# One key tile of 128 rows with quadrant scores, four load buffers, and loads issued two steps further ahead, in an mLSTM and mixture-of-experts kernel

## The chip, the cores and the metric

The kernel runs on one core of one Trainium2 chip. A core has five engines that run their own instruction streams in order: TensorE (PE in the rows; PEld is its weight load), VectorE (DVE), ScalarE (ACT), GpSimd (POOL) and SyncE (SP), which here issues nearly all loads and stores. The metric is the device time of one execution in microseconds (us), lower is better. Times are medians of several runs; the rows come from one profiled execution.

## The reference, cut to what matters

For 4 batches, 8 heads, 768 tokens and a head dimension of 40, a matrix memory is carried from token to token, read with q, gated and normalised. The result, 3072 tokens of 320 features, goes to a mixture of 8 experts where each token takes the one with the largest cosine logit.

```python
for t in range(768):                       # per batch and head
    m_new = max(f[t] + m, i[t])
    C = exp(f[t]+m-m_new) * C + exp(i[t]-m_new) * outer(v[t], k[t])
    n = exp(f[t]+m-m_new) * n + exp(i[t]-m_new) * k[t]
    y[t] = sigmoid(o[t]) * (C @ q[t]) / max(abs(n @ q[t]), 1)
x = y.reshape(3072, 320)                   # heads side by side
logits = unit(x) @ unit(expert_emb).T / tau
e = argmax(logits);  gate = softmax(logits)[e]
out = gate * (relu(x @ w1[e]) @ w2[e])     # w1: 320x1024, w2: 1024x320
```

## The kernel before

The recurrence is computed by chunks of 64 tokens. The loop over n has 24 steps: 6 windows of 128 tokens, each for 4 batches, so one step is 128 tokens of one batch, that is two chunks c of 64 tokens, for 8 heads. Two steps are a pair q and share one load of keys (transposed, `k_e` and `k_o`), one of queries (`q_s`, transposed) and two of rows (`kv_s`, one per step, with keys and values token by token). Each of these has three buffers (NB).

The order of the work is the order of the code, engine by engine; a framework adds only the semaphores. On PE a step n does, in this order:
- stage_add for chunk 0 (L664 carries the state in, L674 adds keys times weighted values) into the PSUM tile `y`. ACT then copies the state between the chunks out of it (`c_mid`, L690, two copies).
- stage_scores of the next step (L637): for each chunk and head a product of 64 keys and 64 queries over 40 dimensions. Heads of even and of odd position sit in two tiles, `k_e` and `k_o`, each of 128 partitions of which 40 are loaded and the rest hold zeros, so that a product over all 128 partitions picks one head out of `q_s`, where two heads sit at partitions 0 to 39 and 64 to 103. The scores `s` of a step fill one PSUM bank; DVE multiplies them with the causal mask into `w_s` (L646).
- stage_y: scores times values (L712), which comes behind ACT's `c_mid` because both touch the bank of `y`; on odd steps five transposes (L792, `px` and `pj`) for the router; and queries times state (L725).
- stage_add for chunk 1 (L674), and on odd steps the logits of an earlier pair (L812, `pm`).

Beside it DVE computes denominators, outputs and the router's argmax in small pieces (L743 to L1009), POOL the weighted values `uv` (L622) and the output gate (L762), ACT copies and squares (L785, L771, L798), and from step 10 on ACT and DVE or POOL split the first expert's weights into two parts (`w1h`, L197, from the loaded tile `raw`). After the loop the mixture of experts (L390, L428) runs, PE-bound, to the end.

Loads are issued in step n by SP in this order: k of pair (n+4)/2 on even steps or q on odd steps, rows, the output gates `sig`, from step 10 on weights `raw` (W_AT), and late in the step the store of an output tile (`x_d`, L766), which waits for POOL's gate. The framework gives the transfers eight semaphores in turn (DMAHW0 to DMAHW7), so each waits until the one eight before it has landed.

Before the loop, the unloaded partitions of six key tiles are zeroed by DVE, POOL and ACT (L1087). PSUM is full: one bank each for `s` (pS), `pj` (pJ) and `px` (pX), two for the router's and the gates' small products (pM), three for `y` (pY).

Of the kernel before, what the change touches and what calls it, by code (L numbers as in the profile page):

```python
# [11 lines left out]
F32 = mybir.dt.float32  # L12
# [11 lines left out]
E, F = 8, 1024  # L24
# [26 lines left out]
W_AT = (10, 12, 13, 15, 16, 18, 19, 20, 22, 22, 22, 23, 23)  # L51
W2_AT = (4, 6, 8, 10, 11, 13, 14)
# [14 lines left out]
def tile_mlstm_moe(  # L67
# [149 lines left out]
    pM = mctx.enter_context(tc.tile_pool(name="pM", bufs=2, space=PSUM))  # L217
# [90 lines left out]
    turns = [(pM, "pm"), (pX, "px")]  # L308
# [229 lines left out]
    with ExitStack() as actx:  # L538
# [7 lines left out]
        pS = ictx.enter_context(tc.tile_pool(name="pS", bufs=1, space=PSUM, side="right"))  # L546
        pJ = ictx.enter_context(tc.tile_pool(name="pJ", bufs=1, space=PSUM, side="right"))

# [12 lines left out]
        NH, NG, NB = B * H, NJ * B * H, 3  # L561
# [11 lines left out]
        k_e, k_o, q_s, kv_s, kr_s, vr_s, uv, w_s = [], [], [], [], [], [], [], []  # L573
        for i in range(NB):
# [5 lines left out]
            vr_s.append(kv_s[i][:, :, :, :, D:])  # L580
            uv.append(ap1.tile([P, 2, NP, 2, D1], F32, name=f"uv{i}"))
            w_s.append(ap1.tile([P, 2, NP, L], F32, name=f"w_s{i}"))
# [11 lines left out]
        def stage_row(q, k, eng=SY):  # L594
            eng.dma_start(
                kv_s[q % NB][:, k].rearrange("p c a d -> p (c a d)"), rows_in[q][:, k].rearrange("p c a d -> p (c a d)")
            )

        def stage_k(q, ks=slice(0, 2)):
            for r, kk in ((0, k_e), (1, k_o)):  # L600
                SY.dma_start(
                    kk[q % NB][r * L : r * L + D, ks].rearrange("d n a t -> d (n a t)"),
                    kt[q, r][:, ks].rearrange("d n a t -> d (n a t)"),
                )

        def stage_q(q, ks=slice(0, 2)):
            SY.dma_start(
                q_s[q % NB][:, ks].rearrange("d n a t -> d (n a t)"), qt[q][:, ks].rearrange("d n a t -> d (n a t)")
# [8 lines left out]
        def stage_uv(n, eng=None):  # L617
            q, k = divmod(n, 2)
            j, b = divmod(n, B)
            for r in range(2):  # L620
# [3 lines left out]
                    vr_s[q % NB][rows, k],  # L624
# [4 lines left out]
        def stage_scores(n):  # L629
            q, k = divmod(n, 2)  # L630
            s = st.setdefault(n, {})["s"] = pS.tile([P, 2, NP, L], F32, name=f"s_{n}", tag="ps")
            for c in range(2):
                cs = slice(c * L, c * L + L)
                for a in range(NP):
                    for r in range(2):
                        m = a // 2 * 2 + r
                        T.matmul(  # L637
                            s[r * L : r * L + L, c, a],
                            (k_e, k_o)[a % 2][q % NB][:, k, m, cs],
                            q_s[q % NB][:, k, m, cs],  # L640
                            start=True,
                            stop=True,
                        )

        def stage_weigh(n):
            V.tensor_tensor(  # L646
                w_s[n % NB].rearrange("p c a t -> p (c a) t"),
                st[n]["s"].rearrange("p c a t -> p (c a) t"),
                late.unsqueeze(1).broadcast_to([P, 2 * NP, L]),
# [6 lines left out]
        def stage_add(n, c):  # L656
# [15 lines left out]
            for a in range(NP):  # L672
# [3 lines left out]
                    kr_s[q % NB][:, k, c, a],  # L676
# [28 lines left out]
        def stage_y(n, mid=None):  # L705
# [4 lines left out]
            for a in range(NP):  # L710
                for c in range(2):
                    T.matmul(  # L712
                        y[c * L : c * L + L, a * 2 * D1 : (a + 1) * 2 * D1],
                        w_s[n % NB][:, c, a],
# [7 lines left out]
            for m in range(NP):  # L722
                for c, state in ((0, c_st[n % B]), (1, c_mid[n % 2])):
                    if n >= B or c:
                        T.matmul(  # L725
                            yp[c * L : c * L + L, m // 2, :, m % 2],
                            q_s[q % NB][:, k, m, c * L : c * L + L],
# [73 lines left out]
        def stage_logits(q):  # L801
# [4 lines left out]
            if b == 0:  # L806
                grp[g] = dict(pm=pM.tile([P, 512], F32, name=f"pm_{g}", tag="pm"))
            xt = st.pop(n)["xt"]
            st.pop(n + 1)
            for c in range(NX):  # L810
                for r0 in (0, L):
                    T.matmul(  # L812
                        grp[g]["pm"][r0 : r0 + L, b * E : (b + 2) * E],
# [23 lines left out]
        def pmv(g, k):  # L837
# [1032 lines left out]
```

## Time and profile before

| what | value |
|---|---|
| device time, median of 3 runs | 327.11 us (326.43 to 327.32) |
| the profiled execution | 328.47 us |
| its span, first to last instruction | 326.7 us |
| PE busy | 307.4 us (94%) |
| DVE, ACT, POOL busy | 217.2, 164.1, 146.4 us |
| DMA: data, mean rate | 58.52 MB, 179 GB/s |

The span is what the page's shares refer to; 1.8 us of the profiled execution lie outside it. "Idle before" of an instruction is the time that its engine stood before it, with the engine or transfer that ended the wait. A group in a timeline (x16) has the time from its first start to its last end; in the chain of waits, pieces that follow each other don't overlap, so their lengths add up. Matmul records: an instruction in 32-bit floats leaves two records, so the 16 products of one step's scores are "x32".

### The profile page before, as it was taken

The numbers are of one execution on the slowest core, as the hardware profiler recorded it, in microseconds if no ns is written. First come the engines' busy times: TensorE is split into PE (matmuls) and PEld (weight loads), VectorE is DVE, ScalarE is ACT, GpSimd is POOL, SyncE is SP. The second block draws the span as 40 slices with busy tenths as digits, with TensorE's granted clock in tenths as the row PEclk, the third lists the DMA queues.
The fourth block names the chain that finished last, engine by engine and source line by source line (L and its number), as shares of the span: only waits on it lengthen the run. The fifth ranks groups of instructions, "written<-read, shape, count | busy, mean of one in ns | idle before, by whom it ended". The sixth has DMA issues, their size and how long they took to land.

```text
span 326.7 us, 9770 instructions
## 1 busy us (share of the span) xinstructions
PE 307.4 (94%) x3769; PEld 290.8 (89%) x3769; DVE 217.2 (66%) x631; ACT 164.1 (50%) x431; POOL 146.4 (45%) x182
## 2 busy tenths in 40 slices
PE   8998999989988879999999999999999999999991
PEld 3787999978876779999999999999999999999990
DVE  5776797897775549796567684574585584766520
ACT  4656556655663695344265463263373463555300
POOL 6659777688784297040635302321251321512121
PEclk9999999999999979999999999999999999999998
DMA  7998797998997523030594964446446465411001
GB/s 228 283 342 252 264 306 238 290 321 272 340 340 219 183 55 113 2 80 3 180 328 168 316 187 134 129 131 191 124 105 247 112 198 198 129 48 42 10 26 33
DMA packets 25101, 58.52 MB, mean 179 GB/s; under 512 B 3707, under 2 KB 10056, under 8 KB 25046
## 3 DMA queue, kind: packets, MB, share of 16 engines
q1 hardware_dynamic: 22166, 48.91, 47.0%
q0 software_dynamic: 2624, 8.48, 8.4%
q8 instruction: 31, 0.51, 0.7%
q10 hardware_dynamic: 256, 0.43, 0.4%
q14 instruction: 24, 0.20, 0.2%
HBM read 49.98 MB, written 8.19 MB: 178 GB/s over the span
## 4 chain that ended last, share of the span: by engine, by line
PE 84%; DVE 4%; DMA 4%; ACT 4%; issue 2%; POOL 1%; POOLq 0%; DVEq 0%; ACTq 0%
PE ph L390 29%; PE po L428 17%; PE s L637 4%; PE po_b L428 4%; PE po_a L428 4%; PE y L712 4%; PE y L674 3%; PE y L725 3%; PE po L415 3%; PE pt L351 2%; PE warm L1078 2%; DMA k_o<-in_kt 2%; PE pm L812 2%; PE px L792 2%; DMA raw<-in_w 2%
## 5 line engine op out<-in xcount | busy, mean ns | idle before, releaser
L447 POOL DMA_INDIRECT out<-ob,ids x20 | 20.3, 1015 | 99.2 <-DVE ob L444 73.7
L622 POOL TENSOR_TENSOR uv<-kv_s,u_t 64x328 f32<-64x328 f32 x47 | 35.3, 751 | 12.7 <-PE y L674 5.4
L428 PE MATMUL po<-w2h,hh 128*128 128x320 f32 x128 | 40.3, 315 | 0.0
L392 ACT ACTIVATE hh<-ph 128x448 fp32r<-128x448 f32 (+2 forms) x48 | 23.7, 493 | 32.7 <-PE ph L390 29.8
L428 PE MATMUL po<-w2h,hl 128*128 128x320 f32 x128 | 39.6, 309 | 0.0
L428 PE MATMUL po<-w2l,hh 128*128 128x320 f32 x128 | 39.5, 309 | 0.0
L394 DVE SCALAR_TENSOR_TENSOR hl<-ph,hh 128x384 fp32r<-128x384 f32 (+1 forms) x48 | 24.5, 511 | 14.6 <-ACT hh L392 12.3
L390 PE MATMUL ph<-xh,w1l 128*128 128x448 f32 (+2 forms) x96 | 32.0, 337 | 0.0
L390 PE MATMUL ph<-xh,w1h 128*128 128x448 f32 (+2 forms) x96 | 32.0, 336 | 0.0
L197 ACT CAST w1h<-raw 128x512 fp32r<-128x512 f32 x48 | 28.9, 616 | 5.4 <-DMA raw<-in_w 4.9
L444 DVE TENSOR_SCALAR ob<-po,gts 128x320 f32<-128x320 f32 x16 | 8.8, 551 | 27.8 <-PE po L428 27.8
L200 DVE TENSOR_TENSOR w2l<-raw,w2h 128x320 fp32r<-128x320 f32 x58 | 26.7, 497 | 0.2
L197 ACT CAST w2h<-raw 128x320 fp32r<-128x320 f32 x64 | 26.1, 461 | 0.0
L637 PE MATMUL s<-q_s,k_e 128*64 128x64 f32 x384 | 24.5, 223 | 1.2 <-DVE w_s L646 1.2
L690 ACT COPY c_mid<-y 40x164 f32<-40x164 f32 x48 | 14.0, 293 | 22.0 <-PE y L674 21.6
L637 PE MATMUL s<-q_s,k_o 128*64 128x64 f32 x384 | 24.5, 222 | 0.5 <-issue 0.5
L390 PE MATMUL ph<-xl,w1h 128*128 128x448 f32 (+2 forms) x96 | 24.6, 337 | 0.0
L312 POOL DMA_INDIRECT xs<-x_d,ids x20 | 21.4, 1070 | 6.9 <-issue 5.5
L200 DVE TENSOR_TENSOR w1l<-raw,w1h 128x512 fp32r<-128x512 f32 x36 | 24.4, 687 | 0.0
L428 PEld LDWEIGHTS po<-w2l,hh 128*128 128x128 f32 x128 | 24.1, 188 | 0.0
L428 PEld LDWEIGHTS po<-w2h,hh 128*128 128x128 f32 x128 | 24.1, 188 | 0.0
L428 PEld LDWEIGHTS po<-w2h,hl 128*128 128x128 f32 x128 | 24.0, 188 | 0.0
(327 smaller groups left out, 922.2 us busy)
## 6 DMA issues: line engine op xcount, KB each, us to landing
raw<-in_w SPq DMA_DIRECT2D x21, 512.0 KB
raw<-in_w SPq DMA_DIRECT2D x32, 320.0 KB
kv_s<-in_rows SPq DMA_DIRECT2D x23, 324.0 KB
q_s<-in_qt SPq DMA_DIRECT2D x11, 512.0 KB
sig<-in_og SPq DMA_DIRECT2D x24, 160.0 KB
x_d<-x SPq DMA_DIRECT2D x24, 160.0 KB
k_e<-in_kt SPq DMA_DIRECT2D x11, 160.0 KB
k_o<-in_kt SPq DMA_DIRECT2D x11, 160.0 KB
```

The costliest lines, as they stand in the source:

```text
L197: A.copy(h, src)
L200: (eng or V).tensor_tensor(lo, src, h.bitcast(F32), ALU.subtract)
L312: G.indirect_dma_start(out=xs[0 : c.shape[0], a, 0:DM], out_offset=None, in_=x_d[0:rows], in_offset=bass.IndirectOffsetOnAxis(ap=c, axis=0 ...
L390: T.matmul(ph, lt, rh, start=i == 0, stop=i == len(ops) - 1)
L392: A.activation(hh, ph, AF.Relu)
L394: V.scalar_tensor_tensor(hl[:, 0:full], ph[:, 0:full], 0.0, hh[:, 0:full].bitcast(F32), ALU.max, ALU.subtract)
L428: T.matmul(po[0 : ts_.stop - ts_.start, 0:DM], lt[f][:, ts_], rh[:, f], start=k == 0, stop=k == len(ops) - 1)
L447: store = G.indirect_dma_start(out=out, out_offset=bass.IndirectOffsetOnAxis(ap=slots, axis=0), in_=ob, in_offset=None, bounds_check=NT - ...
L622: (eng[r] if eng else G).tensor_tensor(uv[n % NB][rows, :, :, r], vr_s[q % NB][rows, k], u_t[rows, j, b].unsqueeze(3).broadcast_to([L, 2, ...
L637: T.matmul(s[r * L : r * L + L, c, a], (k_e, k_o)[a % 2][q % NB][:, k, m, cs], q_s[q % NB][:, k, m, cs], start=True, stop=True,)
L690: A.copy(dst, src)
L712: T.matmul(y[c * L : c * L + L, a * 2 * D1 : (a + 1) * 2 * D1], w_s[n % NB][:, c, a], uv[n % NB][:, c, a].rearrange("p r d -> p (r d)"), s ...
```

## The change

- Keys lie in one tile `k_s` of 128 partitions, two heads at partitions 0 to 39 and 64 to 103 as in `q_s`, loaded by one transfer of 128 rows (512 KB for a pair) in place of two of 40 rows (160 KB each). The host writes zeros into the rows between. The zeroing of the key tiles is gone; the row of zeros for `x_d` comes from `c_mid`.
- A product of the scores takes 64 of the 128 partitions and 64 columns, a quadrant of the array (40 rows of it in use), in place of all partitions and 64 columns. The scores of the heads at the lower and at the upper partitions go to two PSUM banks, and `w_s` has a new order of axes.
- k, q and rows have four buffers (NL = 4). Their loads stand in a list, `ahead`, of which a step issues two, step 0 one, and steps 4 to 7 three each. From step 8 on a load is issued two steps earlier than before; the list ends in step 17 where the last was issued in step 19.
- PSUM: pS has two banks in the loop, pM one. All logits and ranks of the three router groups share one bank, with ranks written over the logits that they replace. After the loop's last step the banks go to pT and pN.

```diff
+MORE_AT = (4, 5, 6, 7)
...
-    pM = mctx.enter_context(tc.tile_pool(name="pM", bufs=2, space=PSUM))
+    pM = mctx.enter_context(tc.tile_pool(name="pM", bufs=1, space=PSUM))
...
-            k_e.append(ap1.tile([P, 2, NP, P], F32, name=f"k_e{i}"))
-            k_o.append(ap1.tile([P, 2, NP, P], F32, name=f"k_o{i}"))
+            k_s.append(ap1.tile([P, 2, NP, P], F32, name=f"k_s{i}"))
...
         def stage_k(q, ks=slice(0, 2)):
-            for r, kk in ((0, k_e), (1, k_o)):
-                SY.dma_start(
-                    kk[q % NB][r * L : r * L + D, ks].rearrange("d n a t -> d (n a t)"),
-                    kt[q, r][:, ks].rearrange("d n a t -> d (n a t)"),
-                )
+            SY.dma_start(
+                k_s[q % NL][:, ks].rearrange("d n a t -> d (n a t)"), kt[q][:, ks].rearrange("d n a t -> d (n a t)")
+            )
...
-            s = st.setdefault(n, {})["s"] = pS.tile([P, 2, NP, L], F32, name=f"s_{n}", tag="ps")
+            s = st.setdefault(n, {})["s"] = pS.tile([P, 2, 512], F32, name=f"s_{n}", tag="ps")
+            sv = s[:, :, 0 : NP * L].rearrange("p h (c i t) -> p h c i t", c=2, i=NP // 2)
             for c in range(2):
                 cs = slice(c * L, c * L + L)
-                for a in range(NP):
-                    for r in range(2):
-                        m = a // 2 * 2 + r
-                        T.matmul(
-                            s[r * L : r * L + L, c, a],
-                            (k_e, k_o)[a % 2][q % NB][:, k, m, cs],
-                            q_s[q % NB][:, k, m, cs],
...
+                for i in range(NP // 2):
+                    for h in range(2):
+                        rows = slice(h * L, h * L + D)
+                        for r in range(2):
+                            m = i * 2 + r
+                            T.matmul(
+                                sv[r * L : r * L + L, h, c, i],
+                                k_s[q % NL][rows, k, m, cs],
+                                q_s[q % NL][rows, k, m, cs],
...
-        V.memset(k_e[0][:, 0], 0.0)
-        G.memset(k_o[0][:, 0], 0.0)
...
-        zero_act(k_e[1])
...
-        zero_act(k_o[1])
...
+        ahead = []
+        for q in range(2, NS // 2):
+            if q > 2:
+                ahead.append(lambda q=q: stage_k(q))
+            ahead.append(lambda q=q: stage_row(q, 0))
+            ahead.append(lambda q=q: stage_q(q))
+            ahead.append(lambda q=q: stage_row(q, 1))
...
-            q = (n + 4 - n % 2) // 2
-            if n and q < NS // 2:
-                (stage_q if n % 2 else stage_k)(q)
-            if q < NS // 2:
-                stage_row(q, n % 2)
+            for _ in range(1 if n == 0 else 3 if n in MORE_AT else 2):
+                if ahead:
+                    ahead.pop(0)()
...
             if n == 0:
                 gates_ends()
-                for t in (k_e[2], k_o[2]):
-                    zero_act(t)
                 stage_k(2)
```

The first place is PE in step 10: the end of its first stage_add, the scores of step 11 and the first part of stage_y. Before:

```order
L674 MATMUL y_1164<-uv_154,kv_s_159 40x82 x3
L637 MATMUL s_1177<-q_s_158,k_e_156 64x64 [waits DVE_49]
L637 MATMUL s_1177<-q_s_158,k_e_156 64x64
L637 MATMUL s_1177<-q_s_158,k_o_157 64x64 x2
L637 MATMUL s_1177<-q_s_158,k_e_156 64x64 x2
L637 MATMUL s_1177<-q_s_158,k_o_157 64x64 x2
L637 MATMUL s_1177<-q_s_158,k_e_156 64x64 x2
L637 MATMUL s_1177<-q_s_158,k_o_157 64x64 x2
L637 MATMUL s_1177<-q_s_158,k_e_156 64x64 x2
L637 MATMUL s_1177<-q_s_158,k_o_157 64x64 x2
L712 MATMUL y_1164<-uv_154,w_s_155 64x82 [waits Activation_49]
L712 MATMUL y_1164<-uv_154,w_s_155 64x82 x7
```

Now, the same work of the same step:

```order
L677 MATMUL y_1150<-uv_158,kv_s_149 40x82 x3
L640 MATMUL s_1163<-q_s_148,k_s_147 64x64 [waits DVE_49]
L640 MATMUL s_1163<-q_s_148,k_s_147 64x64 x15
L715 MATMUL y_1150<-uv_158,w_s_159 64x82 [waits Activation_49]
L715 MATMUL y_1150<-uv_158,w_s_159 64x82 x7
```

No instruction moved here and none fell away: 16 products stand between the same neighbours with waits on the same engines; only their operands and the part of the array that they use have changed.

The second place is SP's queue in steps 4 to 6. Before, where `k_e_150` is pair 4 and `k_e_156` pair 5:

```order
L601 DMA k_e_150<-in_kt 40x1024 [waits DMAHW3_49,PE_49]
L601 DMA k_o_151<-in_kt 40x1024 [waits DMAHW4_49,PE_49]
L595 DMA kv_s_153<-in_rows 128x648 [waits DMAHW5_49,PE_49]
L615 DMA sig_511<-in_og 128x320 [waits DMAHW6_49]
L766 DMA x_d<-x_406 128x320 [waits DMAHW7_49,Pool_49]
L766 DMA x_d<-x_406 128x320 [waits DMAHW0_49,Pool_49]
L607 DMA q_s_152<-in_qt 128x1024 [waits DMAHW1_49,PE_49]
L595 DMA kv_s_153<-in_rows 128x648 [waits DMAHW2_49,PE_49]
L615 DMA sig_511<-in_og 128x320 [waits DMAHW3_49]
L766 DMA x_d<-x_737 128x320 [waits DMAHW4_49,Pool_49]
L601 DMA k_e_156<-in_kt 40x1024 [waits DMAHW5_49,PE_49]
L601 DMA k_o_157<-in_kt 40x1024 [waits DMAHW6_49,PE_49]
```

Now, in the same steps, where `k_s_144` is pair 4 and `k_s_147` pair 5:

```order
L602 DMA k_s_144<-in_kt 128x1024 [waits DMAHW6_49,PE_49]
L597 DMA kv_s_146<-in_rows 128x648 [waits DMAHW7_49,PE_49]
L607 DMA q_s_145<-in_qt 128x1024 [waits DMAHW0_49,PE_49]
L615 DMA sig_498<-in_og 128x320 [waits DMAHW1_49]
L769 DMA x_d<-x_394 128x320 [waits DMAHW2_49,Pool_49]
L769 DMA x_d<-x_394 128x320 [waits DMAHW3_49,Pool_49]
L597 DMA kv_s_146<-in_rows 128x648 [waits DMAHW4_49,PE_49]
L602 DMA k_s_147<-in_kt 128x1024 [waits DMAHW5_49,PE_49]
L597 DMA kv_s_149<-in_rows 128x648 [waits DMAHW6_49,PE_49]
L615 DMA sig_498<-in_og 128x320 [waits DMAHW7_49]
L769 DMA x_d<-x_725 128x320 [waits DMAHW0_49,Pool_49]
L607 DMA q_s_148<-in_qt 128x1024 [waits DMAHW1_49,PE_49]
```

The two transfers of k have become one, q of pair 4 has moved from step 5 to step 4 and k of pair 5 from step 6 to step 5, each ahead of stores and gates that stood before it.

## Rows read from the trace of the kernel before

**Rows 1.** The page's second part: busy tenths of PE and of the DMA engines in 40 equal slices of the span (8.2 us each).

```profile
PE   8998999989988879999999999999999999999991
...
DMA  7998797998997523030594964446446465411001
```

**Rows 2.** Windows: for each stretch (us from the span's start) its length, the busy time and instructions of each engine, the granted PE clock, the DMA engines' busy share and what they moved.

```profile
46.00:58.00 12.00, 12.00 (x315) 11.19 (x311) 9.23 (x38) 7.46 (x23) 8.03 (x10) 1.00 0.81 258
58.00:76.00 18.00, 16.68 (x425) 15.29 (x425) 16.18 (x49) 10.62 (x32) 14.06 (x17) 1.00 0.94 309
76.00:96.00 20.00, 18.36 (x478) 17.05 (x475) 15.27 (x55) 12.58 (x38) 15.96 (x20) 1.00 0.99 326
96.00:110.00 14.00, 11.09 (x239) 9.59 (x235) 8.29 (x28) 7.18 (x23) 5.50 (x7) 1.00 0.73 238
```

**Rows 3.** The chain of waits that ended last in the stretch from 36 to 58 us, in order of time: start, length, what.

```profile
42.69 0.54 PE pm L812 x20
...
43.82 0.93 PE s L637 x32
44.75 0.57 PE y L712 x16
...
46.74 0.93 PE s L637 x32
```

**Rows 4.** Timeline of PE from 53.9 us, one step, and one row from 71.7 us: start, length from first start to last end, engine, line, operation, out<-in, tile and shape, count, and in brackets idle time before and what ended it.

```profile
54.25 0.28 PE L637 MATMUL s<-q_s,k_e 128*64 128x64 f32 x4
...
55.18 0.74 PE L712 MATMUL y<-uv,w_s 128*64 128x82 f32 x16
55.85 0.66 PE L792 MATMUL px<-ident,xc 128*128 128x128 f32 x4
56.35 0.27 PE L792 MATMUL pj<-ident,xc 128*128 128x128 f32 x1
56.55 0.28 PE L725 MATMUL y<-c_st,q_s 128*64 128x82 f32 x1
56.56 0.28 PE L725 MATMUL y<-c_mid,q_s 128*64 128x82 f32 x1
...
71.74 0.79 PE L712 MATMUL y<-uv,w_s 128*64 128x82 f32 x16 [0.51 <-ACT c_mid L690]
```

**Rows 5.** Timeline of ACT, columns as in rows 4, from the same step, and around 70 us.

```profile
54.46 0.60 ACT L690 COPY c_mid<-y 40x164 f32<-40x164 f32 x2 [1.43 <-PE y L674]
...
70.45 0.62 ACT L197 CAST w1h<-raw 128x512 fp32r<-128x512 f32 x1 [1.11 <-DMA raw<-in_w]
71.09 0.59 ACT L690 COPY c_mid<-y 40x164 f32<-40x164 f32 x2
```

**Rows 6.** PE's groups by line and shape between 36 and 58 us: records, busy time (of pipelined records, so it adds up to more than the engine's), mean ns of one record.

```profile
L637 PE MATMUL s<-q_s,k_o 128*64 128x64 f32 x96 | 5.9, 222 | 0.0
...
L812 PE MATMUL pm<-ent,xt 128*64 128x16 f32 x60 | 2.1, 206 | 0.0
```

**Rows 7.** The waits: of all PE between 30 and 112 us, of ACT between 58 and 96 us, of SP's queue between 58 and 76 us. Engine and line, what it waited for, us in total, times, the longest.

```profile
PE y L712 <- ACT c_mid L690: 2.2, 4, 0.8
...
ACT w1h L197 <- DMA raw<-in_w: 4.9, 5, 1.8
...
SPq L615 <- DMA k_e<-in_kt: 0.2, 1, 0.2
```

**Rows 8.** The chain of waits that ended last in the stretch from 58 to 72 us.

```profile
58.81 6.43 DMA k_o<-in_kt
...
65.26 5.17 DMA raw<-in_w
```

**Rows 9.** SP's issues between 56 and 72 us: start and length of the issue, line, transfer.

```profile
58.35 0.36 SPq L601 DMA_DIRECT2D k_e<-in_kt  x1
58.81 0.33 SPq L601 DMA_DIRECT2D k_o<-in_kt  x1
...
64.28 0.33 SPq L615 DMA_DIRECT2D sig<-in_og  x1
```

**Rows 10.** The chain of waits that ended last in the stretch from 84 to 100 us; an "issue" piece is time in which PE waited for nothing that the profile shows.

```profile
86.04 0.53 issue
...
92.08 0.61 issue
...
93.17 0.94 PE s L637 x32
94.12 0.03 issue
94.14 0.69 DVE w_s L646
...
97.44 1.47 issue
```

**Rows 11.** Timeline of DVE from 76 us.

```profile
76.74 0.69 DVE L646 TENSOR_TENSOR w_s<-s,late 128x512 f32<-128x512 f32 x1 [0.53 <-PE s L637]
```

**Rows 12.** The chain of waits that ended last in the stretch from 8 to 20 us.

```profile
9.41 1.15 PE s L637 x32
...
14.43 1.08 PE s L637 x32
```

**Rows 13.** Timeline of ACT from 0 to 13 us, one of its four zeroings of a key tile.

```profile
3.07 1.04 ACT L1087 ACTIVATE k_e<-onef 128x1024 f32<-128x1024 f32 x1
```

More of the change, by code (lines that the diff above doesn't have):

```diff
@@ L545, in tile_mlstm_moe @@
         ap = ictx.enter_context(tc.tile_pool(name="ap", bufs=2, side="right"))
-        pS = ictx.enter_context(tc.tile_pool(name="pS", bufs=1, space=PSUM, side="right"))
         pJ = ictx.enter_context(tc.tile_pool(name="pJ", bufs=1, space=PSUM, side="right"))
+        sctx = ExitStack()
+        pS = sctx.enter_context(tc.tile_pool(name="pS", bufs=1, space=PSUM, side="right"))
         rs = ss_all
@@ L571, in tile_mlstm_moe @@
         stage_gates(0)
-        k_e, k_o, q_s, kv_s, kr_s, vr_s, uv, w_s = [], [], [], [], [], [], [], []
-        for i in range(NB):
-            k_e.append(ap1.tile([P, 2, NP, P], F32, name=f"k_e{i}"))
-            k_o.append(ap1.tile([P, 2, NP, P], F32, name=f"k_o{i}"))
+        k_s, q_s, kv_s, kr_s, vr_s, uv, w_s = [], [], [], [], [], [], []
+        for i in range(NL):
+            k_s.append(ap1.tile([P, 2, NP, P], F32, name=f"k_s{i}"))
             q_s.append(ap1.tile([P, 2, NP, P], F32, name=f"q_s{i}"))
@@ L580, in tile_mlstm_moe @@
             vr_s.append(kv_s[i][:, :, :, :, D:])
+        for i in range(NB):
             uv.append(ap1.tile([P, 2, NP, 2, D1], F32, name=f"uv{i}"))
-            w_s.append(ap1.tile([P, 2, NP, L], F32, name=f"w_s{i}"))
+            w_s.append(ap1.tile([P, 2, 2, NP // 2, L], F32, name=f"w_s{i}"))
         c_st = [ap1.tile([P, NP, 2 * D1], F32, name=f"c_st{b}") for b in range(B)]
@@ L623, in stage_uv @@
                     uv[n % NB][rows, :, :, r],
-                    vr_s[q % NB][rows, k],
+                    vr_s[q % NL][rows, k],
                     u_t[rows, j, b].unsqueeze(3).broadcast_to([L, 2, NP, D1]),
@@ L713, in stage_y @@
                         y[c * L : c * L + L, a * 2 * D1 : (a + 1) * 2 * D1],
-                        w_s[n % NB][:, c, a],
+                        w_s[n % NB][:, a % 2, c, a // 2],
                         uv[n % NB][:, c, a].rearrange("p r d -> p (r d)"),
@@ L805, in stage_logits @@
             b = n - GROUPS[g][0]
-            if b == 0:
-                grp[g] = dict(pm=pM.tile([P, 512], F32, name=f"pm_{g}", tag="pm"))
+            if not grp:
+                pm = pM.tile([P, 512], F32, name="pm", tag="pm")
+                grp.update({i: dict(pm=pm) for i in range(len(GROUPS))})
             xt = st.pop(n)["xt"]
@@ L835, in nt, with pmo, pmv @@
             return GROUPS[g][1] - GROUPS[g][0]
-        def pmv(g, k):
+        def pmo(g):
+            return sum(nt(i) * E + E * NTT + E for i in range(g))
+        def pmv(g):
             w = nt(g) * E
-            return grp[g]["pm"][:, k * w : (k + 1) * w].rearrange("p (t e) -> p t e", e=E)
+            return grp[g]["pm"][:, pmo(g) : pmo(g) + w].rearrange("p (t e) -> p t e", e=E)
         def pids(g):
-            return grp[g]["pm"][:, 2 * nt(g) * E : 2 * nt(g) * E + E * NTT]
+            at_ = pmo(g) + nt(g) * E
+            return grp[g]["pm"][:, at_ : at_ + E * NTT]
         def ohg(g):
@@ L1004, in cntv @@
         def cntv(g):
[L1005 removed]
+            at_ = pmo(g + 1) - E
+            return grp[g]["pm"][:, at_ : at_ + E]
         def early_count():
@@ L1102, in tile_mlstm_moe @@
         V.memset(onef, 1.0)
-        V.memset(k_e[0][:, 1], 0.0)
         V.memset(ones[:, 1:], 1.0)
@@ L1270, in embeddings @@
                 V.tensor_scalar(en, en, ens, taub[:E], ALU.mult, ALU.mult)
-                zrow = flat(k_e[2])[P - 1 : P]
+                zrow = c_mid[0].rearrange("p m d -> p (m d)")[P - 1 : P]
                 SY.dma_start(x_d[PAD : PAD + 1], zrow[:, 0:DM])
@@ L1373, in tile_mlstm_moe @@
                 route(n, 0)
+                sctx.close()
+                pT = ictx.enter_context(tc.tile_pool(name="pT", bufs=2, space=PSUM, side="right"))
             turn = None
@@ L1476, in tile_mlstm_moe @@
         yctx.close()
+        pN = mctx.enter_context(tc.tile_pool(name="pN", bufs=1, space=PSUM))
+        turns.append((pN, "pn"))
         pH = mctx.enter_context(tc.tile_pool(name="pH", bufs=3, space=PSUM))
@@ L1591, in tile_mlstm_moe @@
     hs = hidden("b")
-    banks += [(pH, "ph")] * 2 + [(pM, "pm")] * 2
+    banks += [(pH, "ph")] * 2 + [(pM, "pm"), (pN, "pn")]
     for e in range(NE):
```

53 lines of the change are left out of this document (21 added, 32 removed).

## The prediction

> **What bounds the kernel now.** I read the page's strip of slices first [rows 1]: PE is busy at nine tenths or more in nearly every slice, and the DMA engines at nine tenths or more only in stretches of the first hundred microseconds. So I read the first 110 us by windows [rows 2]. From 46 to 58 us PE has no idle time at all. From 58 to 110 us it idles 1.3, 1.6 and 2.9 us (length less busy time), 5.9 us together, and there the DMA engines are busy to 94 and 99% and then 73%. After 110 us PE runs the experts, which the change leaves as they are. The kernel is thus bound by PE's own sequence, and by DMA where transfers come too late. I then read the chain of waits in each kind of stretch: in the unstalled one it is PE alone, with a block of scores (L637) of 0.93 us in each step [rows 3].
>
> **Scores in quadrants.** Sixteen products stay sixteen, 32 records, 0.93 us or 29 ns a record [rows 3]. The logits, with 16 moving columns in place of 64 and the same 64 columns of weights, take 0.54 us for 20 records, 27 ns [rows 3, 6]: it isn't the moving columns that set the rate but what each record brings with it, its weights above all. Today two column halves of the array work side by side. If four quadrants do, the block takes half, 0.47 us; if they don't, 0.93. Added are two changes of the array's mode a step, into quadrants and back to L712's halves. The price of such a change is read at the transposes, which use the whole array: the 16 records of L712 need 0.57 us [rows 3], so the last ends its turn at 55.18 + 0.57 = 55.75 and `px` starts at 55.85, 0.10 later; out of the whole array, `pj` starts at 56.35 and L725 at 56.55 [rows 4], 0.20, of which 0.12 is the transpose's own turn (four in 0.50 us), so 0.08. I take 0.1 a change, 0.2 a step. The block with its changes is then 0.67 or 1.13 us against 0.93. I take the small end, since the records in the two halves start 0.01 us apart where they don't use the same part (56.55 and 56.56) [rows 4].
>
> [...]
>
> What comes of a shorter block? L712 must wait for ACT's `c_mid` too, which starts at 54.46 behind stage_add and ends at 55.06; L712 starts at 55.18 [rows 4, 5]. In a stalled step it starts at 71.74, with `c_mid` over at 71.68, so 0.06 behind it [rows 4, 5]. Were the scores free, L712 would start at 55.06 + 0.06 = 55.12. A step gains 0.06 us at most, in 18 such steps (5 to 22) 1.1 us, and as PE would idle briefly and start anew there, I put it at **0**, with bounds from -1.1 to +3.6 (18 x 0.2, the block not shorter and the changes in full).
>
> Two early blocks stand on the path with little beside them, 1.15 us at 9.41 and 1.08 at 14.43 [rows 12]. Each gains 0.26 by the forecast: **-0.5** (bounds -0.9, if halved without changes, and +0.4). DVE waits for scores on the path too: `w_s` at 76.74 waited 0.53 for L637, and at 94.14 L637 (93.17) with `w_s` behind it leads into the router's chain [rows 10, 11]. Each starts 0.26 earlier: **-0.5** (bounds -0.9, +0.4).
>
> **Zeroing.** Four copies of about a microsecond on ACT [rows 13] and four fills on DVE and POOL go. In this stretch PE and DVE's gate chain set the pace [rows 12], and ACT's first zeroing runs while the gates' loads are under way: 0. The cover is the gate chain; were it gone, one zeroing, 1.0 us, is the most to gain.
>
> **PSUM.** The banks of the router groups fall together. Logits now wait for DVE's earlier reads of the same bank, and those lie a group or a step back in DVE's order: 0. pX takes over no new work in the loop. If a read were late, `pm` would wait for some 0.5 us twice, within the range.
>
> **k in one transfer.** What does k cost the DMA queue today? Each issue on SP waits for the transfer eight before. `sig` at 64.28 is eight behind `k_e`, and SP's waits name `k_e` as its releaser [rows 7, 9]; so `k_e` had landed at about 64.28, and `k_o` landed at 58.81 + 6.43 = 65.24 [rows 8]: 0.96 us for 160 KB, where the mean rate of 318 GB/s in the busy windows [rows 2] would give 0.52. The pair takes 1.92 us. One transfer of 512 KB takes 1.65 at that rate: 0.27 less. The opposite bound is by bytes alone: 192 KB more a pair, 0.62 us at 318 GB/s. That pays where a weight is late: `k_o`, then `raw`, then ACT's cast at 70.45, `c_mid`, and L712 at 71.74 [rows 5, 8]. ACT waits 4.9 us for `raw`, but its slack takes most of that: PE waits 2.2 us for `c_mid` behind it [rows 7]. With two k pairs ahead of the late casts, and SP held less by full buffers, I take **-0.9**, between 0 and -2.2; by bytes it is 2 x 0.62 = +1.2.
>
> **Loads two steps further ahead.** k, q and rows are hardly waited for by PE today, so an earlier load by itself gains nothing. What is gained is that the list is empty two steps sooner: its last pair (324 KB twice, 512 KB of q, 512 of k), 1.7 MB, leaves the full window from 76 to 96 us for the time from step 4 on, where the engines have room (81% busy from 46 to 58) [rows 2]. That is over 5 us of a full queue. Three pieces in which PE waits for nothing shown, 0.53, 0.61 and 1.47 us, 2.6 together, stand where the DMA engines are at 99%, and the page has a queue of instruction fetches among the DMAs; I put them down to fetches that queue behind data. With the list over by then I take half: **-1.3** (bounds -2.6 and, with k's bytes, +0.6) [rows 2, 10].
>
> In steps 4 to 7 SP issues one load more each, ahead of `sig` and of stores. A load is an issue of 0.35 us [rows 9] and up to 512 KB, 1.65 us, ahead of `sig`; the sigmoid on ACT is what comes late next, then `c_mid`. One such step held by the whole transfer would cost about 1.5. PE and ACT have slack there (ACT idled 1.43 us before `c_mid`) [rows 5]: **+0.3** (bounds 0, +1.5).
>
> **The sum** is 0 - 0.5 - 0.5 - 0.9 - 1.3 + 0.3 = -2.9 us, made against the profiled execution's 328.47 us: 325.6. That execution lies 1.4 us above the median of the runs, 327.11, and the same difference gives **324.2**.
>
> **The rivals.**
> *Slower by quadrants.* Place: each step's L637 to L712. If the quadrants run one after another, every step pays 0.2 for the two changes: +3.6, with +0.4 at each of the early and the DVE places; -0.9, -1.3 and +0.3 stay. Sum +2.5: 329.6. It decides from where block and changes exceed 0.93, a block of 0.73 us. The equal rate of scores and logits [rows 3, 6] speaks for it, as far as a record has a price that parts of the array can't share; the starts 0.01 us apart speak against it. [...]
> *Nothing comes of the queue.* k's added bytes eat what one transfer saves, raw +0.8, fetches 0: -0.5 - 0.5 + 0.8 + 0.3 = +0.1, so 327.2. For it: a queue at 99% counts bytes. Against: 1.92 us for 320 KB.
> *All late transfers vanish.* Raw -2.2 and fetches -2.6 with the rest as summed but no cost in steps 4 to 7: -5.8, so 321.3. For it: 5 us of load leave the full window. Against: weights still queue there.
> *The shorter block shows in every step.* 18 x 0.26 = 4.7 off on top of the forecast: 319.5. Against it stands `c_mid`, ready only 0.12 us before L712 starts today.
> *The change doesn't act:* loads still wait for their buffers. The order shows the waits on PE kept, but for a buffer that is free a pair sooner; this falls with the second rival.
>
> **How the numbers follow.** Chances: forecast 0.45, slower by quadrants 0.17, nothing from the queue 0.14, all late transfers vanish 0.12, the shorter block shows 0.08, and 0.04 for k's bytes outweighing all (raw +1.2, fetches +0.6, loads +1.5 against -1.0: +2.3, 329.4). A measurement of this kernel can tell about 0.3%, 1.0 us, from no change. Faster by more than that: 0.45 + 0.12 + 0.08 = 0.65; within it 0.14; slower 0.17 + 0.04 = 0.21. The range goes from 320.0 to 329.5: it leaves out the last fast rival and the upper part of the slow ones. The forecast's own range is 322.0 to 326.0.
>
> **What would show it.** In the profile after, the score block's length in the chain (0.47 plus about 0.1 on either side, or over 0.9), and L712's start 0.06 behind `c_mid` with an idle note. The waits of ACT for `raw` below 3 us, and the issue pieces behind 84 us at about half; the DMA share of the last window lower and that of 32 to 58 us higher. If PE idles before L674 or L725 for `kv_s` or `sig`, the extra loads cost more than said. The prediction is wrong if the block with its changes of mode stays above 0.93 us, or if the idle of PE from 58 to 110 us doesn't fall from 5.9 to some 3.5 us.

## The result, and the profile after

The changed kernel takes 329.08 us (median of 4 runs, 328.58 to 329.24) against 326.89 us of the kernel before in the same session: 1.0065 times as long, with a 95% interval of 1.0046 to 1.0083. It is slower by 2.2 us where 2.9 us less were forecast. A ratio, here and below, is taken over the runs within 1.5% of the fastest of their kernel; medians under the experiments are of all runs.

The score block did what the forecast took. These rows are of the timeline of PE of the changed kernel (columns as in rows 4), one step from 49.5 us, to be read beside rows 4:

```profile
49.53 0.69 PE L640 MATMUL s<-q_s,k_s 40*64 40x64 f32 x32
50.30 0.79 PE L715 MATMUL y<-uv,w_s 128*64 128x82 f32 x16
...
53.85 0.34 PE L640 MATMUL s<-q_s,k_s 40*64 40x64 f32 x8
```

One record lasts 0.22 us, so the starts of the 32 lie within 0.47 us, 15 ns from one to the next; in the block of the kernel before that starts at 54.25 they lie within 0.88, 28 ns. With two quadrants at most at a time the block takes 0.98 us (halves in turn, below) in place of 0.69, so I read this as four quadrants working side by side. L715 starts 0.77 us after the block's first record, before 0.93 [rows 4], but the next block starts 4.32 us after this one, before 4.34 (from 46.74 in rows 3 to the next block of that chain, the first row below). What holds L715 is the row behind it, from the timeline of ACT of the changed kernel:

```profile
51.08 0.93 PE s L637 x32
```

```profile
49.65 0.60 ACT L693 COPY c_mid<-y 40x164 f32<-40x164 f32 x2 [3.07 <-PE y L677]
```

`c_mid` is over at 50.25 and L715 starts 0.05 later: it waits for `c_mid` as it was forecast to.

The loss is in the middle of the loop. Windows of the changed kernel (columns as in rows 2):

```profile
32.00:46.00 14.00, 11.61 (x297) 9.88 (x291) 8.83 (x37) 7.90 (x24) 9.18 (x13) 0.98 1.04 398
46.00:58.00 12.00, 11.78 (x287) 10.43 (x288) 8.96 (x33) 5.65 (x18) 7.16 (x10) 0.88 0.73 256
58.00:76.00 18.00, 16.63 (x425) 14.38 (x427) 16.41 (x48) 12.28 (x37) 13.04 (x15) 1.00 0.97 334
76.00:96.00 20.00, 19.30 (x522) 16.76 (x516) 18.36 (x60) 13.04 (x39) 17.34 (x21) 1.00 0.78 268
```

The DMA view of the changed kernel between 32 and 46 us; a queue's row has its packets, MB and share of the 16 engines:

```profile
DMA packets 2529, 5.58 MB, mean 398 GB/s; under 512 B 281, under 2 KB 1219, under 8 KB 2524
...
q8 instruction: 2, 0.03, 0.8%
```

The same stretch of the kernel before:

```profile
DMA packets 1893, 3.87 MB, mean 276 GB/s; under 512 B 223, under 2 KB 1032, under 8 KB 1889
```

Between 32 and 46 us PE had no idle time before (14.00 us busy, DMA share 0.85); now it is idle 2.4 us, with 1.7 MB more moved and the DMA engines full. Between 76 and 96 us it is the other way round: their share fell from 0.99 to 0.78 and PE's idle time from 1.6 to 0.7 us [rows 2]. What PE waited for in the middle, from the timeline of PE of the changed kernel:

```profile
39.02 0.56 PE L640 MATMUL s<-q_s,k_s 40*64 40x64 f32 x19 [0.42 <-issue]
...
45.65 0.37 PE L640 MATMUL s<-q_s,k_s 40*64 40x64 f32 x1 [1.90 <-issue]
...
47.09 0.35 PE L728 MATMUL y<-c_st,q_s 128*64 128x82 f32 x1
...
47.23 0.34 PE L728 MATMUL y<-c_st,q_s 128*64 128x82 f32 x1
...
51.91 0.24 PE L728 MATMUL y<-c_st,q_s 128*64 128x82 f32 x1
...
51.98 0.23 PE L728 MATMUL y<-c_st,q_s 128*64 128x82 f32 x1
```

The timeline of ACT of the changed kernel there:

```profile
37.81 0.47 ACT L739 ACTIVATE sig<-sig 128x320 f32<-128x320 f32 x1 [1.16 <-DMA sig<-in_og]
...
46.11 0.47 ACT L739 ACTIVATE sig<-sig 128x320 f32<-128x320 f32 x1 [1.39 <-DMA sig<-in_og]
```

PE stops in the middle of a block, between two records of one line, waiting for nothing that the profile shows ("issue"). After the second stop records of L728 follow each other by 0.14 us, where they do by 0.07 from 51.91 on: the granted clock is at half for 3.4 us, from 45.6 to 49.0 (mean 0.88 from 46 to 58 us, 1.00 before). ACT gets `sig` late, which it never waited for in these steps before.

What ends such a stop can be read from the single DMA packets, which the trace holds with start and length. The queue q8, an instruction queue by the page, moved 31 packets of 16 KB in the profile of the changed kernel as in that of the kernel before, where PE has 7622 and 7620 records (matmuls, weight loads and 84 and 82 of its sequencer), 246 to a packet. And the stops stand whole multiples of 256 such records apart: here behind 1474, 1730 and, at 72.45 us, 3010, in the kernel before behind 3778, 4034 and 4290. From both I take a packet to hold 256 of PE's instructions. The packet ahead of the stop that ends at 45.65 landed at 44.04. In the thirteen traces of the table below, all 53 stops of PE of 0.2 us or more between 20 and 99 us that the profile calls "issue" end 1.2 to 1.6 us after such a packet landed (1.26, 1.61 and 1.42 in the changed kernel), though one starts only every 5.4 us there on the mean. I read these stops as waits for instructions. The packet comes late because its start does: from the first of these places to the start of the next packet it took 4.1 us (39.01 to 43.16), in the kernel before, behind as many records, 1.6 (39.66 to 41.28), and PE didn't stop.

The second new wait is at the loop's end. Timeline of PE of the changed kernel where the first expert's tokens are transposed (`pa`) and its first products (`ph`) begin:

```profile
109.85 0.66 PE L367 MATMUL pa<-ident,xs_a 128*128 128x128 f32 x4 [0.85 <-ACT xs_a L343]
112.42 0.36 PE L391 MATMUL ph<-xh_a,w1h 128*128 128x256 f32 x1 [1.91 <-DVE xt_a L372]
```

And of the kernel before:

```profile
109.67 0.87 PE L366 MATMUL pa<-ident,xs_a 128*128 128x128 f32 x6
111.12 0.39 PE L390 MATMUL ph<-xh_a,w1h 128*128 128x256 f32 x1 [0.58 <-ACT xh_a L368]
```

`ph` waited 0.58 us for ACT and now waits 1.91 for DVE's last read of `pa`: with the banks as they are now, the pool of `ph` begins on banks that held `pa`.

### The profile page after: what moved, and what is told of

The parts are those of the page before. It is cut to its first block, busy times and chain, and to the rows that moved or that the text cites. A ratio compares the mean times of both kernels' runs of the same rounds, so it can differ in the third digit from the quotient of the medians.

```text
span 327.5 us, 9736 instructions
## 1 busy us (share of the span) xinstructions
PE 304.3 (93%) x3769; PEld 283.4 (87%) x3769; DVE 217.8 (66%) x629; ACT 160.6 (49%) x427; POOL 145.4 (44%) x180
## 4 chain that ended last, share of the span: by engine, by line
PE 61%; DVE 2%; ACT 1%; issue 0%; POOL 0%; POOLq 0%; ACTq 0%
PE ph L391 29%; PE po L429 17%; PE po_b L429 4%; PE po_a L429 4%; PE po L416 3%; PE pt L352 2%; DVE w2l L201 1%; ACT w1h L198 1%; PE pg L520 0%; DVE hl_a L395 0%; PE px L795 0%; POOL out L448 0%; PE pa L367 0%; DVE ob L445 0%; POOLq L1656 0%
## 5 line engine op out<-in xcount | busy, mean ns | idle before, releaser
L715 PE MATMUL y<-uv,w_s 128*64 128x82 f32 x384 | 19.8, 245 | 3.3 <-ACT c_mid L693 2.1
L677 PE MATMUL y<-uv,kv_s 128*40 128x82 f32 x352 | 21.7, 237 | 0.7 <-issue 0.7
```

The lines of the kernel that those rows point to most:

```text
L677: T.matmul(pc[r0 : r0 + D, m : m + 2], kr_s[q % NL][:, k, c, a], uv[n % NB][:, c, a], start=n < B and c == 0 and a < 2, stop=True, skip_gr ...
L715: T.matmul(y[c * L : c * L + L, a * 2 * D1 : (a + 1) * 2 * D1], w_s[n % NB][:, a % 2, c, a // 2], uv[n % NB][:, c, a].rearrange("p r d -> ...
```

## Theories

A: the third loads of steps 4 to 7 fill the DMA queue, so that PE's instructions and `sig` come late; that is the loss. B: the 192 KB more of k per pair are. C: the banks at the loop's end are. D: gains ahead of step 21 are lost behind it, where gathered tokens are waited for. E: the short block makes PE's clock fall more easily. F: late instructions matter only with the quadrants' faster block.

A measure for A that later stops don't touch is the time from the first score record of step 0 to that of step 13 in a timeline of PE. Two executions of the kernel before, in different sessions, agree in it within 0.14 us, while from step 13 to step 21 they differ by 1.5. All starts stand in the traces; the kernels are described below, in the order of the DMA share.

| kernel | DMA share 32 to 46 us | scores 0 | scores 13 | 0 to 13 | 13 to 21 | time, ratio to before (95%) |
|---|---|---|---|---|---|---|
| old cadence and banks | 0.80 | 7.27 | 58.73 | 51.46 | 34.63 | 0.9964 (0.9922 to 1.0007) |
| before | 0.85 | 7.33 | 58.59 | 51.26 | 34.38 | 1 |
| before again | 0.85 | 6.75 | 57.87 | 51.12 | 32.92 | 0.9981 (0.9940 to 1.0022) |
| no third loads | 0.87 | 6.63 | 58.05 | 51.42 | 34.41 | 1.0028 (0.9999 to 1.0057) |
| transposes ahead | 0.88 | 6.97 | 57.96 | 50.99 | 35.45 | 0.9957 (0.9920 to 0.9993) |
| spread and banks | 0.91 | 6.65 | 59.44 | 52.79 | 34.40 | 1.0058 (1.0025 to 1.0091) |
| spread | 0.95 | 7.01 | 59.17 | 52.16 | 36.54 | 0.9998 (0.9967 to 1.0030) |
| prefetch only | 0.98 | 7.20 | 62.28 | 55.08 | 32.76 | 1.0054 (1.0020 to 1.0087) |
| two k transfers | 0.99 | 6.56 | 60.80 | 54.24 | 32.14 | 1.0051 (1.0019 to 1.0083) |
| sig first | 1.03 | 7.24 | 61.86 | 54.62 | 34.71 | 1.0028 (0.9999 to 1.0057) |
| halves in turn | 1.03 | 7.20 | 60.45 | 53.25 | 32.84 | 1.0034 (1.0001 to 1.0067) |
| after | 1.04 | 6.71 | 61.49 | 54.78 | 31.92 | 1.0065 (1.0046 to 1.0083) |
| banks | 1.04 | 6.63 | 59.97 | 53.34 | 33.11 | 1.0026 (0.9989 to 1.0062) |

Up to a share of 0.88 the stretch takes 51.0 to 51.5 us, at 0.91 and 0.95 it takes 52.2 to 52.8, and from 0.98 on 53.3 to 55.1. Each row is one execution. Halves in turn is a case apart: its stops in this stretch are 0.6 us together, and most of its 2 us is a slower block. And a full queue doesn't always stop PE. Old cadence and banks has one from 46 to 58 us, with no such stop there; the first, of 0.39 us, ends at 59.68:

```profile
46.00:58.00 12.00, 11.79 (x315) 10.22 (x313) 9.19 (x37) 7.41 (x23) 8.02 (x11) 1.00 0.98 332
```

## Experiments

**No third loads.**

```diff
-MORE_AT = (4, 5, 6, 7)
+MORE_AT = ()
```

> The changed kernel, but no step issues a third load (MORE_AT empty), so k, q and rows are issued in the same steps as before the change, with four buffers, one k transfer and quadrants kept. Theory A (the third loads of steps 4 to 7 fill the DMA queue, an instruction fetch of PE comes late in step 9, PE stands 1.9 us and runs at half clock after): no issue stall near 45 us, no half clock there, 1.5 to 4 us less than the changed kernel, 325 to 327.5. Theory B (the 192 KB more per pair of the 128-row k are the cause): the queue is as full, 328.5 to 329.5. Theory C (the banks at the loop's end are the cause, 0.6 to 2 us): no change here.

1.0028, median 327.69 us. The stop near 45 us is down to 0.26 us, the first row here, and ACT no longer waits for `sig`; the stretch to step 13 is back at 51.4. The time doesn't fall clearly to that of before: fetches now stop PE later, the second row, and by 1.31 us at 70.46.

```profile
43.76 0.27 PE L640 MATMUL s<-q_s,k_s 40*64 40x64 f32 x1 [0.26 <-issue]
...
98.04 0.58 PE L715 MATMUL y<-uv,w_s 128*64 128x82 f32 x10 [1.61 <-issue]
```

**Third loads spread.**

```diff
-MORE_AT = (4, 5, 6, 7)
+MORE_AT = (5, 8, 11, 14)
```

> The changed kernel with the four third loads spread: steps 5, 8, 11 and 14 in place of 4 to 7. Theory A: the queue between 32 and 46 us stays below the saturation of the changed kernel, the stall of step 9 shrinks below 0.6 us and the half clock there goes: 325 to 327.5. Theory B and C: 328.5 to 329.5.

0.9998, median 327.01 us. The stop of step 9 fell to 0.53 us, but there was a longer one, 768 instructions on, where the share was 0.97 (46 to 58 us) and 0.94 (58 to 76):

```profile
61.70 0.46 PE L640 MATMUL s<-q_s,k_s 40*64 40x64 f32 x14 [1.98 <-issue]
```

**k by two transfers.** The edit without its rearrangements of axes:

```diff
-            SY.dma_start(k_s[q % NL][:, ks], kt[q][:, ks])
+            for r in range(2):
+                rows = slice(r * L, r * L + D)
+                SY.dma_start(k_s[q % NL][rows, ks], kt[q][rows, ks])
```

> The changed kernel with k loaded by two transfers of 40 rows (160 KB each) into the one tile, the zero rows not loaded; quadrants, four buffers and third loads kept. Theory A: the bytes of the stretch from 32 to 46 us fall by about 0.6 MB of 5.6, the stall in step 9 may shrink but one more transfer a pair is in the queue: 327 to 329.5. Theory B: 2 to 4 us less, 325 to 327.

1.0051: the fewer bytes don't help, the DMA share is still 0.99 (347 GB/s in place of 398). B falls as the main cause.

**Banks of ph.**

```diff
+        pH = mctx.enter_context(tc.tile_pool(name="pH", bufs=3, space=PSUM))
         pN = mctx.enter_context(tc.tile_pool(name="pN", bufs=1, space=PSUM))
         turns.append((pN, "pn"))
-        pH = mctx.enter_context(tc.tile_pool(name="pH", bufs=3, space=PSUM))
```

> The changed kernel with the pool of the experts' first products (pH) opened ahead of pN, so that pH takes the banks of y and not a bank that held the first expert's transposed tokens. Theory C: the first matmul of L391 no longer waits for DVE's xt_a (1.91 us of idle before it), it starts some 1 us earlier, and the half clock behind it may go: 327 to 328.5. Theories A and B alone: no change, 329.

1.0026. The wait is the old one again, here in this kernel's timeline of PE:

```profile
110.03 0.66 PE L367 MATMUL pa<-ident,xs_a 128*128 128x128 f32 x4 [1.49 <-ACT xs_a L343]
111.27 0.58 PE L391 MATMUL ph<-xh_a,w1h 128*128 128x256 f32 x1 [0.58 <-ACT xh_a L369]
```

From the second `pa` group to `ph` it takes 1.24 us, in the changed kernel 2.57: the order of two pools is worth 1.3 us at this place. What reaches the end isn't settled. The hope that the clock would stay up behind `ph` failed: it is at its lower level from 110.6 to 117.5 us here, in the changed kernel from 113.8 to 117.3. Of three pairs that differ by the order alone, after and banks, no third loads and old cadence and banks, spread and spread and banks, two fell (by 0.4 and 0.6%) and one rose (by 0.6%), each pair measured in two sessions.

**Loads of before with the quadrants.** Both of the first and third edits.

> The changed kernel with the loads of before: no third loads, and k by two transfers of 40 rows. What is left of the change is the quadrants, their banks, no zeroing and the fourth buffer. Theory A (the earlier loads make the stalls): the loss is gone, 325 to 327. Theory C (banks at the loop's end) and theory D (what is gained ahead of step 21 is lost behind it, where the experts' first products wait for gathered tokens): 326.5 to 328. Theory E (the short score block lets PE stand or run thin in each step, and PE's granted clock falls more easily at a stall): mean granted clock below the 0.987 of the kernel before, 327 to 329.

1.0001 (0.9967 to 1.0035). The loss is gone with the loads, and nothing is gained. Its profiled execution took 333.75 us, far above its median of 328.36, and is not used.

**The kernel before again.**

> The kernel before, unchanged, for a second profile. All theories: 324 to 329, as its runs. It tells which stalls of the first profile stand in each execution: theory D wants the first experts' products (L390) to wait for gathered tokens here too; if the issue stalls at 86, 92 and 97 us lie elsewhere or have other lengths, single stalls are no property of a kernel.

0.9981. The same 51.1 us to step 13; then other stops than in the first profile. `ph` waits 0.58 us for ACT here too and not for gathered tokens, against D; in the changed kernel `pa` waits 0.85 for them, so a part of D may hold there, and no run here tells how much.

**Halves in turn.** The loop over h is outermost, so that two quadrants at most work at a time.

```diff
-            for c in range(2):
-                for i in range(NP // 2):
-                    for h in range(2):
+            for h in range(2):
+                for c in range(2):
+                    for i in range(NP // 2):
```

> The changed kernel with the 16 quadrant products in another order: all of the lower partitions first, then all of the upper, so that only two quadrants can work at a time. The price of a score block whose quadrants don't work side by side: 0.93 us and two changes of mode, L715 later by 0.1 to 0.2 a step. Without theory E: 330 to 333, granted clock as the changed kernel. Theory E: PE has no gap in front of L715, the granted clock rises to 0.99 and the time stays at 328 to 330.

1.0034, neither expectation's time. In its timeline of PE:

```profile
36.27 0.98 PE L640 MATMUL s<-q_s,k_s 40*64 40x64 f32 x32
37.18 0.79 PE L715 MATMUL y<-uv,w_s 128*64 128x82 f32 x16
```

L715 starts 0.91 us after the block, against 0.77 with four quadrants: the price that the slow rival stood on is 0.14 us a step here, about 2.5 us in 18 steps, and yet the kernel isn't slower than the changed one. Its stops up to step 13 were smaller (0.21 us at step 9). With a slower PE a fetch has more time, which may be why; no run separates that.

**Spread and banks**, both remedies.

> The changed kernel with third loads in steps 5, 8, 11 and 14 and pH opened ahead of pN, both remedies together. Theories A and C: their gains add, 325 to 326.5. Theory D or E: no better than either alone, 326.5 to 328.5.

1.0058: the gains don't add, though `ph` waits 0.58 us as expected and the stop of step 9 is 0.53. The kernel before ranges over 5 us and more in a session, so a ratio says no more than its interval, and why this one is slow isn't shown.

**Old cadence and banks.** No third loads, and pH ahead of pN.

> The changed kernel without third loads and with pH opened ahead of pN. Theory A (third loads fill the queue): no loss between the scores of steps 0 and 13 against the kernel before (51.3 us there). Theory C adds an L391 that doesn't wait for xt_a. If both hold: 0.995 to 1.000 of the kernel before. If the 512 KB k is a cost by itself: above 1.003.

0.9964, interval up to 1.0007; one of its 12 executions took 648.0 us and is left out. The profiled execution had a mean clock of 0.993 with the short block in each step, the kernel before again 0.991, so the block need not bring the clock down. E isn't ruled out by that. Over all runs this kernel's mean granted clock is level with that of the kernel before in its session (0.991), but in the nine other versions with quadrants it is lower, by 0.001 to 0.011, while prefetch only, with the long block and late fetches, is level (0.992 against 0.991). A mean lower by 0.005 is 3.3 us at half clock in 327, up to 1.6 us of time, an estimate; that isn't small beside what is at stake here.

**Prefetch only.** The kernel before, with four buffers and the list, nothing else.

```diff
+MORE_AT = (4, 5, 6, 7)
...
-        NH, NG, NB = B * H, NJ * B * H, 3
+        NH, NG, NB, NL = B * H, NJ * B * H, 3, 4
...
+            for _ in range(1 if n == 0 else 3 if n in MORE_AT else 2):
+                if ahead:
+                    ahead.pop(0)()
```

> The kernel before with nothing but the earlier loads: four buffers of k_e, k_o, q and rows, and the list with third loads in steps 4 to 7; scores, k's two tiles and their zeroing as before (a fourth pair is zeroed too). Theory A: the DMA share between 32 and 46 us rises from 0.85 to 0.95 or more, sig comes late on ACT, and from the scores of step 0 to those of step 13 it takes 52.5 us or more against 51.3; 1.002 to 1.008. Theory F (it takes the quadrants, whose block runs through its instructions faster, to make a late fetch count): 51.3 to 51.8 there and 0.993 to 1.000.

1.0054 (1.0020 to 1.0087), 55.1 us to step 13 in place of 51.3: the earlier loads alone bring the whole loss of this stretch, without quadrants, bank changes or a larger k. Its waits of ACT between 25 and 60 us (us in total, times, the longest):

```profile
ACT sig L738 <- DMA sig<-in_og: 5.2, 3, 2.6
```

And two rows of its timeline of PE:

```profile
46.23 0.27 PE L639 MATMUL s<-q_s,k_o 128*64 128x64 f32 x1 [1.05 <-issue]
49.95 0.79 PE L714 MATMUL y<-uv,w_s 128*64 128x82 f32 x16 [0.53 <-ACT c_mid L692]
```

The stop stands at the same place of the program, in the scores of step 9, and `sig` is late. For the stretch to step 13 A is shown and F falls.

**Transposes ahead.** Old cadence and banks, and on odd steps:

```diff
+            if mid and n > 5:
+                mid()
+                mid = None
             for a in range(NP):
...
-            stage_mid(n)
             if n > 5:
                 stage_xc(n - 2)
+            stage_mid(n)
+            if n > 5:
                 stage_sq(n - 2)
```

> As the kernel with old cadence and banks, and on odd steps from 7 on the transposes px and pj stand between the scores and L715, with ACT's copy xc ahead of c_mid, so that PE has work while c_mid is made. If the quadrants' gain lies hidden under c_mid, as the prediction has it, odd steps get 0.15 to 0.3 us shorter (4.34 before): 0.990 to 0.997. If xc comes late, c_mid does too, and odd steps get longer: 1.000 to 1.005.

0.9957 (0.9920 to 0.9993), the one version that is faster than the kernel before beyond its interval. Its timeline of PE:

```profile
46.59 0.69 PE L640 MATMUL s<-q_s,k_s 40*64 40x64 f32 x32
47.22 0.66 PE L798 MATMUL px<-ident,xc 128*128 128x128 f32 x4
...
50.62 0.58 PE L640 MATMUL s<-q_s,k_s 40*64 40x64 f32 x24
```

This odd step takes 4.03 us in place of 4.32. The quadrants' gain was hidden under `c_mid` and shows in the step once PE has other work there; the same order with the old block wasn't run. In the time it doesn't show: old cadence and banks, which differs by this alone, has 0.9964 in the same session, and the median of all 12 runs is 327.16 us against 327.46 of the kernel before.

**Sig first.** The loop that issues `sig` stands ahead of the list's loads.

> The changed kernel with the output gates' loads (sig) issued ahead of the step's other loads; third loads stay. Theory A, the part by sig: ACT waits less than 1 us for sig between 25 and 60 us (3.1 in the changed kernel) and half of the loss up to step 13 goes: 1.001 to 1.005. If the fetch alone makes the loss: sig no longer late, and the loss as before, 1.004 to 1.008.

1.0028. ACT no longer waits for `sig` between 25 and 60 us, but the stretch to step 13 still takes 54.6 us, with a stop of 1.6 us in a score block and, in its timeline of PE, another in which PE waits 1.59 us with DVE named as the releaser. The row behind it is that instruction in the timeline of DVE:

```profile
57.69 0.69 PE L640 MATMUL s<-q_s,k_s 40*64 40x64 f32 x32 [1.59 <-DVE ge L954]
```

```profile
56.43 0.37 DVE L954 TENSOR_TENSOR ge<-rk_all,thr 128x30 f32<-128x30 f32 x1
```

DVE was done at 56.80, 0.89 us before PE went on, so it isn't what PE waited for last. The place lies 512 instructions behind the stop of step 9, and a fetch packet landed at 56.18, 1.5 us before the restart: this is a fetch too. With 0.4 us of smaller ones, such stops are 3.6 us of this stretch, as much as the loss. So `sig` is not the larger part; with the queue as full as before, late fetches alone can make up the loss here.

## Why the prediction was wrong

The step that failed is the price of the third loads: "**+0.3** (bounds 0, +1.5)" for steps 4 to 7. Measured it is 3.4 us from step 0 to step 13 against the same kernel without them (54.78 against 51.42), 3.5 against the kernel before (51.26, with the front's gain inside it), and 3.8 alone (prefetch only). The reasoning behind it failed in two places. It took the share of 0.81 from 46 to 58 us for room, while the loads came together from 32 to 46 us, where the share was 0.85: 1.7 MB more there is nearly half of what was moved before, and filled the queue. And it counted late instruction fetches as something that the change takes away from the full window after 76 us, not as something that the full queue which it makes would bring: one stop of 1.90 us, with the clock at its lower level after it, is larger than the whole bound. The two stops up to step 13 are 2.3 us of the loss; the 3.4 us at half clock are at most 1.7 more, an estimate.

Only a part of this is lost in the end. From step 13 to 21 the third loads give back 2.5 us (31.92 against 34.41 without them), so they and the late window cost 0.9 together where -1.0 was forecast, 1.9 of the 5.1 us between forecast and result. Between 20 and 99 us the stops of PE called "issue" add up to 3.1 us in the changed kernel and to 2.6 in each profile of the kernel before: the change moved them more than it added to them. The profile after (span 327.5 us) is longer than the two before (326.7 and 324.1) by 0.8 and 3.4 us, shared out as follows (rounded): ahead of step 0 by -0.6 and 0.0, to step 13 by 3.5 and 3.7, to step 21 by -2.5 and -1.0, behind it by 0.4 and 0.8. What else was lost can't be shared out so finely. Without the third loads and with `ph` on other banks the kernel has 0.9964, 1.2 us less than before, and the terms that are left, -1.9 us, lie within its interval.

That the stated range, up to 329.5 us, holds 329.08 is luck: its upper end came from quadrants that run in turn and from k's bytes, and neither is what happened.

The other steps:
- Quadrants side by side, and 0 gained in the steady step: right, 4.32 against 4.34 us, and hidden by `c_mid` as said; the block takes 0.47 us from first to last start.
- What sets a record's rate: that it is above all the weights, as the prediction had it, was an inference from two near rates (29 and 27 ns), and no run shows it. Measured are starts 28 ns apart in the block before (0.88 us over 31 intervals) and 15 ns in quadrants (0.47 us).
- The front, -0.5: right. From the scores of step 0 to those of step 4 (21.83 before, 20.62 after) it takes 13.91 us against 14.50.
- The three pieces put down to fetches: right, each ends 1.5 us after a fetch packet landed. But the longest, at 97.44, isn't where the DMA engines are at 99%: that window ends at 96, and from 97 to 99 us their share is 0.51.
- The late window, -1.3: right in kind. From step 13 to 21 it takes 31.92 us against 34.38 and 32.92 in the two executions before, and no stop of 0.2 us or more called "issue" is left from 84 to 100 us. PE's idle time from 58 to 110 us fell from 5.9 to 4.9 us, not to the 3.5 that the prediction had set itself.
- k, -0.9: not shown. ACT's waits for `raw` fell from 4.9 to 3.5 us, not below 3, but they are 1.7 in the second execution of the kernel before, and two transfers in place of one made no difference that can be told. The term was sized from one execution. ACT between 58 and 96 us, the changed kernel and the kernel before again:

```profile
ACT w1h L198 <- DMA raw<-in_w: 3.5, 4, 1.7
```

```profile
ACT w1h L197 <- DMA raw<-in_w: 1.7, 1, 1.7
```

- PSUM, 0: wrong at its place. The loop's banks cost nothing, but the banks after the loop put 1.3 us in front of `ph`. The prediction looked for new waits inside the loop only.
- DVE, -0.5: not told apart from the stops around it.

The prediction also took quadrants in turn, its slow rival, for the likeliest way to lose. That price is real but small (halves in turn), and the loss came from elsewhere.

## What to carry to other kernels

Here the earlier loads were not free: 1.7 MB more between 32 and 46 us took the DMA share from 0.85 to 1.04 and the stretch to step 13 from 51.3 to 54.8 us. So look for room in the very stretch into which a load moves: add its bytes to that window's megabytes and compare with the rate of a full window of the same kernel (398 GB/s at a share of 1.04 here), ahead of asking which tensor comes late. PE's instructions came by DMA too (queue q8 of the page, 31 packets of 16 KB), and in these traces a full queue went with stops of PE, 0.2 to 2.0 us, at places that have no wait in the program: look for stops that lie multiples of one number of instructions apart (256 here), each soon behind the landing of a fetch packet (1.2 to 1.6 us here). Putting `sig` first didn't mend it (54.6 us to step 13). The block shorter by 0.16 us up to L715 gave 0.02 us a step behind the wait for `c_mid`; with the transposes moved into that gap an odd step took 4.03 us in place of 4.32, if not yet less time. And a term read from one execution can be the accident of that execution (ACT waited 4.9 us for `raw` in one of the kernel before and 1.7 in the other): profile the kernel before twice.

## What had not been expected of the hardware

- The DMA engines moved 398 GB/s over 14 us, where the fullest window of rows 2 had 326.
- PE's stops without a wait in the program lie whole multiples of 256 records apart (1474, 1730 and 3010 in the changed kernel), and 31 packets of 16 KB came on the fetch queue. At a DMA share of 1.04 a packet started 4.1 us behind such a place, at 0.85 1.6 us; the stops of 0.2 us or more last up to 2.0, and PE goes on 1.2 to 1.6 us after a packet landed.
- Single executions of one kernel differ by several us: in the session of the first four experiments the kernel before ranged from 323.98 to 328.79 us in 35 runs. Stops for fetches don't explain that by themselves: they are 2.6 us in both profiles of the kernel before, which are 2.6 us apart in span.
